# K's rows from split sums, the FFN gate's row inside the first block, and splits and copies at other places, in an adaLN, S4 and SwiGLU kernel

## The chip, the cores and the metric

The kernel runs on one core of one Trainium2 chip. The core has five engines with a queue of instructions each: TensorE (PE, matmuls; its weight loads are shown as PEld), VectorE (DVE), ScalarE (ACT), GpSimd (POOL) and SyncE (SP), which here only issues transfers. The metric is the device time of one execution in microseconds (us), the median of several runs. Matmuls write to PSUM, which is used here as eight banks of 128 x 512 fp32.

## The reference

One layer: an adaptive layer norm, a state space convolution (S4), a second adaptive layer norm and a SwiGLU FFN, with two residual sums. L = 2048 tokens, D = 448 channels, N = 256 states, F = 1792 hidden channels, all in fp32.

```python
mod = (_silu(c) @ w_mod).reshape(c.shape[0], 6, 1, -1)
sa, ca, ga, sb, cb, gb = (mod[:, 0], mod[:, 1], mod[:, 2], mod[:, 3], mod[:, 4], mod[:, 5])
h = _layernorm(x, axis=-1) * (1 + ca) + sa
x = x + ga * _A_ref(h, ...)      # y = conv(h, K) + h * Dskip, K[d, l] = Re sum_n C exp(dt A l) dt B
h = _layernorm(x, axis=-1) * (1 + cb) + sb
x = x + gb * ((_silu(h @ w_gate) * (h @ w_up)) @ w_down)
```

## The kernel before

**Method.** Where the exponents `dt A l` are small enough, K[d, l] is taken as a straight line in l: a value `m0` and a slope `m1` for each channel, both multiplied by the gate `ga`. The convolution is then two running sums over the tokens, made by matmuls with triangular matrices, and a sum carried from tile to tile in `run`. A flag computed from the states picks this path; otherwise a general path runs, which these inputs do not take.

**Precision.** A fp32 matmul runs as two records in the trace. Where that is too dear, an operand is split into a high part rounded to fp32r and a low part (the rest, also in fp32r), and the product is three fp32r matmuls of one record each: high x high, high x low, low x high. ACT makes the high part (a cast), DVE the low one (a subtraction).

**Stages.** The tokens are 16 tiles of 128, in blocks of 2, 2, 3, 3, 3, 3 tiles (`BLOCKS`). An opening stage prepares everything and makes the first two tiles ready; then for each block `ffn` runs over 14 slices f of the hidden channels. A step f is `gate_up(f)`, 22 matmuls (L724), and then `down(f - 1)`, 6 or 9 matmuls (L768). Its other work: `p`, the silu on ACT (L739); the product of gate and up on DVE (L752); its high part `phi` on ACT (L755) and its low part `plo` on DVE (L756). In the first block (`fresh`) the weights of the slices are split while it runs: `split_d(f)` (L112; ACT L115, DVE L117) and, with `nw`, `split_w(f + 2)` in three pieces (L119; ACT L123, DVE L125 and L127), mixed with the rest of the step.

**Order.** Each engine runs its instructions strictly in the order in which the program issues them. In the opening this order is written out by hand: `PLAN` is a list of short names, each standing for a function in `todo`, and `ORDER` is the order of the transfers that SP issues (s: states, m: columns of `w_mod`, x: tiles of tokens, w and d: weights of FFN slices). The names of `PLAN` that matter here:

- `pa`, `ps`: rows of the modulation as matmuls with c spread over 128 rows (`mod_part`). `gp`, `cp`, `sp`, `gq`: the same in four groups of 32 columns (`mod_quads`). `gt`, `gac`: the gate `ga` turned into columns.
- `S1`, `S20`, `S21`, `S3` (ACT), `a2`, `a3` (DVE): sums over the states. `t1` to `t5`, `wr`, `wi`: the products they need. `m0`, `dg`, `gdm` (POOL), `m1`: combining and gating them.
- `k0`, `k1`, `gdr`: the columns `m0`, `m1` and the skip `gdm` spread into rows by `row_of` (L348), matmuls against the unit matrix; `gd` copies the last.
- `h..`, `v0.`, `v1.`, `hd.`: the first norm of tiles 0 and 1 and its products with the rows; `o..`: the matmuls that sum them (`o00` to `o02` tile 0, `o10` to `o14` tile 1; `far` and `ramp` are constant matrices); `xh1`, `x1`: tile 1's residual.
- `st`, `r`, `n1.`, `xn`: the second norm of the two tiles (statistics on DVE, root on POOL L167 and L168, scaling on DVE and ACT). `tr`: its transposes, `hi` and `lo`: its split (ACT L428, DVE L433). `sbt`, `sbc`: the shift `sb` as columns, needed by `hi`.
- `l1`, `lr0`, `lr1`: the sum left over for the next tile; `lr1` ends with a transfer that ACT issues (L410, L411). `x0`: a copy of tile 0's residual.
- `gq`, `gqc`, `gbk`, `gb`: the gate row of the FFN: four groups, copied, summed and spread over 128 rows by one matmul with `pick` (`spread_row`, L381), copied to `gb`.
- `w0..`, `w1..`, `w2..`, `d0.`, `d1.`: splits of the first weights.

**In the blocks.** `TIMES` says at which half step (2f before `down`, 2f + 1 after it) the pieces of the next block's tiles are issued: for blocks 0 and 1 the last two entries are the root of the second norm and, per tile, `make_xn` (L189: DVE L193, ACT L194 and L195). At the end of a block the transposes of the next tiles (L206) follow the matmuls of f = 13 on PE.

Of the kernel before, what the change touches and what calls it, by code (L numbers as in the profile page):

```python
# [51 lines left out]
def f32(ap):  # L52
    return ap.bitcast(F32)
# [3 lines left out]
def tile_kernel(ctx, tc, x, a_re, a_im, b_re, b_im, c_re, c_im, log_dt,  # L57
# [13 lines left out]
    def bank():  # L71
        t = psg.tile([128, 512], F32, name="bank")
        return t
# [160 lines left out]
    def mod_part(ps, w, ks):  # L234

        for k in ks:
            if k < 3:
                pe.matmul(ps[:, 0:D], cs[:, k:k + 1].to_broadcast([128, 128]), w[:, k * D:(k + 1) * D],  # L238
                          start=k == 0, stop=False)
            else:  # L240
                for z in range(2):
                    pe.matmul(ps[:, z * D // 2:(z + 1) * D // 2], cs[:, 3 + z:4 + z].to_broadcast([128, 128]),
                              w[:, 3 * D:NM], start=False, stop=z == 1)

    def mod_quads(ps, w):

        for k in range(3):
            pe.matmul(ps[32 * k:32 * k + 32, 0:D], cs[:, k:k + 1].to_broadcast([128, 32]), w[:, k * D:(k + 1) * D],
                      start=True, stop=True)
        for z in range(2):  # L250
            pe.matmul(ps[96:128, z * D // 2:(z + 1) * D // 2], cs[:, 3 + z:4 + z].to_broadcast([128, 32]), w[:, 3 * D:NM],
                      start=z == 0, stop=z == 1)

    def to_dram(row, col):
# [12 lines left out]
    with tc.tile_pool(name="pre", bufs=1) as pre:  # L267
# [3 lines left out]
        wms, S = {5: m5.rearrange("p a b -> p (a b)")}, {}  # L271
# [32 lines left out]
        ident2 = pre.tile([128, 64], F32)  # L304
# [31 lines left out]
        qt = {n: pre.tile([128, D], F32, name="qt" + n) for n in "gcsb"}  # L336
        gdm = pre.tile([128, 4], F32, name="gdm")
        t_, WV = f32(tri), ve
# [8 lines left out]

        def row_of(m, ps, last=ident2):  # L348

            for k in range(4):  # L350
                n = 128 if k < 3 else 64
                pe.matmul(ps[:, k * 128:k * 128 + n], m[:, k:k + 1].to_broadcast([128, 128]), ident if k < 3 else last,
                          start=True, stop=True)
            return ps[:, 0:D]
# [3 lines left out]
        def row(g, z):  # L358

            if z == 0:  # L360
                psm[g] = bank()
            mod_part(psm[g], wms[g], (0, 1) if z == 0 else (2, 3))
# [21 lines left out]
        def gd_row():  # L384
            psm["d"] = bank()
            row_of(gdm, psm["d"], ident[:, 0:64])

        def scaled(o, a, b):
            po.tensor_tensor(o, a, b, op=OP.add)
            po.tensor_tensor(o, o, gac, op=OP.mult)  # L390

        def gated_dt():
            po.tensor_tensor(dt2, dt2, gac, op=OP.mult)
            po.tensor_tensor(ndt2[:, 2:4], ndt2[:, 2:4], gac[:, 2:4], op=OP.mult)
            po.tensor_tensor(a2[:, 0:2], a2[:, 0:2], gac[:, 0:2], op=OP.mult)
# [29 lines left out]
        def high(q):  # L425
            for k in range(4):
                c_ = slice(q * 128, (q + 1) * 128)
                sc.activation(hhi[:, k, c_], pk[q][:, k * 128:(k + 1) * 128], AF.Identity, bias=sbc[:, k:k + 1])  # L428
# [16 lines left out]
        def flag_of():  # L445
# [18 lines left out]
            "m0": do(scaled, m0, m0, m0_), "m1": add(m1, a1, a2), "dg": gated_dt, "k0": do(row_of, m0, CV), "k1": do(row_of, m1, DN[2]),  # L464
            "gdm": mul(gdm, vec[:, 8:12], gac, po), "gdr": gd_row, "gd": copy(gd, lambda: psm["d"][:, 0:D]),

            **{f"{n}{z}": do(row, g, z) for n, g in (("pa", 1), ("ps", 0)) for z in range(2)},
            **{n: do(quads, n[0] if n[1] == "p" else "b", g) for n, g in (("gp", 2), ("cp", 4), ("sp", 3), ("gq", 5))},
            **{n + "c": (lambda c, b: lambda: sc.copy(qt[c], psm[c][:, 0:D]))(c, b) for n, c, b in
               (("gp", "g", 0), ("cp", "c", 0), ("sp", "s", 0), ("gq", "b", 0))},  # L470
# [5 lines left out]
            "gbk": do(spread_row, "b"), "gb": copy(gb, lambda: psm["b"][:, 0:D]),  # L476
# [4 lines left out]
            **{f"hd{q}": mul(hd[q], h01[q], gd, po) for q in range(2)},  # L481
# [9 lines left out]
            **{f"tr{q}": do(to_channels, q) for q in range(2)}, **{f"hi{q}": do(high, q) for q in range(2)},  # L491
# [5 lines left out]
            "w2": do(split_w, 2, 0), "w21": do(split_w, 2, 1), "w22": do(split_w, 2, 2),  # L497
            **{f"d{j}{z}": do(split_d, j, z) for j in range(2) for z in range(2)},
# [201 lines left out]
    def run_blocks(pools, stages, first=None):  # L700
        work, hid = pools.work, pools.hid
        def ffn(ts, fresh, last, todo):
# [4 lines left out]
            def gate_up(f, nw):  # L707
                head = fresh and f == 0
                if fresh and f > 1:
                    split_d(f)  # L710
# [4 lines left out]
                ps = [DN[2] if head else bank(), bank()]  # L715
# [95 lines left out]
            for f in range(NF):  # L811
                gate_up(f, f + 2 if fresh and f and f + 2 < NF else None)
                if fresh:
                    pools.load(f + 2 + NS if f else NF, f + NS)
                if last and f in (2, 4):
                    gated(NF - 2 + (f == 4))
                for g, a in todo.get((f, 0), []):
                    g(*a)
                if f and not (last and f == NF - 1):
                    down(f - 1, qz)  # L820
                if last and f == NF - 2:
                    last_sums()
                for g, a in todo.get((f, 1), []):
                    g(*a)
# [8 lines left out]
        for j in range(NP0, NP0 + NS):  # L833
            pools.load(j)
# [10 lines left out]
        for b, ts in enumerate(TILES):  # L845
            todo = {}
            if b + 1 < len(TILES):
# [152 lines left out]
    with cond.Else():  # L1000
        y = general_conv()
        with ExitStack() as es:
            pools = Pools(es)
            run_blocks(pools, *general_path(pools, y))
# [60 lines left out]
```

## Time and profile before

| | |
|---|---|
| median of 3 runs | 488.02 us (487.7 to 488.93) |
| the profiled execution's own time | 489.08 us |
| its span, from the first instruction to the last | 487.3 us |
| PE busy | 474.4 us (97%) in 2743 matmul records |
| DVE busy | 284.7 us (58%) |
| ACT busy | 155.9 us (32%) |
| POOL busy | 60.8 us (12%) |
| clock granted to TensorE, mean | 0.996 |

A row of the timeline has the start and the length in us, the engine, the line of the kernel, the operation, the tile written and the tiles read, the shape, and how many like it were merged; in brackets the idle time of the engine before it and what ended it. A row of the chain of waits has start, length, engine, tile and line. An `x2` behind fp32 matmuls is one product in two records. The ends of matmuls are modelled, so the start-to-start distance of records tells their price better than their length.

### The profile page before, as it was taken

The numbers are of one execution on the slowest core, as the hardware profiler recorded it, in microseconds if no ns is written. First come the engines' busy times: TensorE is split into PE (matmuls) and PEld (weight loads), VectorE is DVE, ScalarE is ACT, GpSimd is POOL, SyncE is SP. The second block draws the span as 40 slices with busy tenths as digits, with TensorE's granted clock in tenths as the row PEclk, the third lists the DMA queues.
The fourth block names the chain that finished last, engine by engine and source line by source line (L and its number), as shares of the span: only waits on it lengthen the run. The fifth ranks groups of instructions, "written<-read, shape, count | busy, mean of one in ns | idle before, by whom it ended". The sixth has DMA issues, their size and how long they took to land.

```text
span 487.3 us, 7022 instructions
## 1 busy us (share of the span) xinstructions
PE 474.4 (97%) x2743; PEld 447.1 (92%) x2743; DVE 284.7 (58%) x549; ACT 155.9 (32%) x336; POOL 60.8 (12%) x83
## 2 busy tenths in 40 slices
PE   6998999999999999999999999999999999999996
PEld 4667988999998999999999999999999999999995
DVE  4978999577886446565654656264476635222225
ACT  4875555432225212232212133231222231211111
POOL 1231000000000040410004121002241000000000
PEclk9998999999999999999999999999999999999999
DMA  8953752030000200011120011130001112000001
GB/s 309 406 212 110 244 188 87 16 96 1 0 3 2 94 1 0 31 35 49 56 76 1 2 43 45 43 114 0 2 0 45 44 43 77 22 1 0 1 1 62
DMA packets 18778, 31.24 MB, mean 64 GB/s; under 512 B 2608, under 2 KB 13488, under 8 KB 18736
## 3 DMA queue, kind: packets, MB, share of 16 engines
q1 hardware_dynamic: 18000, 30.52, 18.4%
q8 instruction: 23, 0.38, 0.3%
q10 hardware_dynamic: 736, 0.19, 0.2%
q14 instruction: 19, 0.16, 0.1%
HBM read 24.61 MB, written 6.03 MB: 63 GB/s over the span
## 4 chain that ended last, share of the span: by engine, by line
PE 90%; DMA 3%; DVE 3%; ACT 2%; issue 1%; SPq 0%; ACTq 0%; DVEq 0%
PE bank L724 57%; PE dn L768 27%; DMA wm<-in_w_mod_groups_dram 2%; DMA x<-in_A_u_dram 1%; ACT raw L195 1%; PE dn L454 1%; PE bank L238 1%; PE bank L928 1%; PE cv L927 0%; DVE gu L125 0%; PE cv L929 0%; ACT gu L123 0%; DVE raw L193 0%; PE bank L206 0%; DVE hlo L433 0%
## 5 line engine op out<-in xcount | busy, mean ns | idle before, releaser
L724 PE MATMUL bank<-hhi,gu 128*128 128x384 f32 (+1 forms) x1169 | 212.4, 320 | 2.0 <-ACT gu L123 1.4
L724 PEld LDWEIGHTS bank<-hhi,gu 128*128 128x128 f32 x1169 | 192.0, 189 | 5.5 <-ACT gu L123 1.6
L724 PE MATMUL bank<-hlo,gu 128*128 128x384 f32 (+1 forms) x668 | 132.5, 320 | 0.0
L724 PEld LDWEIGHTS bank<-hlo,gu 128*128 128x128 f32 x668 | 110.7, 189 | 0.0
L752 DVE TENSOR_TENSOR bank<-raw,bank 128x384 f32<-128x384 f32 (+1 forms) x69 | 36.9, 534 | 125.0 <-PE bank L724 122.7
L755 ACT CAST phi<-bank 128x384 fp32r<-128x384 f32 (+1 forms) x83 | 36.9, 444 | 144.2 <-DVE bank L752 144.2
L739 ACT ACTIVATE raw<-bank 128x384 f32<-128x384 f32 (+1 forms) x70 | 32.9, 470 | 122.9 <-PE bank L724 114.8
L756 DVE TENSOR_TENSOR plo<-bank,phi 128x384 fp32r<-128x384 f32 (+1 forms) x83 | 42.5, 512 | 37.5 <-ACT phi L755 37.5
L768 PE MATMUL dn<-wdh,phi 128*128 128x448 f32 x218 | 58.3, 369 | 0.0
L768 PE MATMUL dn<-wdh,plo 128*128 128x448 f32 x218 | 57.7, 366 | 0.0
L768 PE MATMUL dn<-wdl,phi 128*128 128x448 f32 x218 | 57.6, 365 | 0.0
L768 PEld LDWEIGHTS dn<-wdl,phi 128*128 128x128 f32 x218 | 41.0, 188 | 3.5
L768 PEld LDWEIGHTS dn<-wdh,plo 128*128 128x128 f32 x218 | 40.9, 188 | 3.3
L768 PEld LDWEIGHTS dn<-wdh,phi 128*128 128x128 f32 x218 | 39.0, 189 | 2.1 <-ACT run L951 0.7
L167 POOL TENSOR_SCALAR rsb<-mvb 128x1 f32<-128x1 f32 (+2 forms) x13 | 4.6, 354 | 172.2 <-DVE mvb L151 170.5
L167 POOL TENSOR_SCALAR rsa<-mva 128x3 f32<-128x3 f32 (+1 forms) x6 | 1.4, 233 | 120.9 <-DVE mva L151 120.9
L123 ACT CAST gu<-raw 128x1024 fp32r<-128x1024 f32 x14 | 14.6, 1044 | 1.1 <-DVE run L410 1.1
L125 DVE TENSOR_TENSOR gu<-raw,gu 128x768 fp32r<-128x768 f32 x14 | 13.3, 953 | 1.8 <-ACT gu L123 1.8
L916 DVE TENSOR_TENSOR vl<-m,vh 128x448 fp32r<-128x448 f32 x12 | 9.1, 757 | 6.7 <-ACT vh L915 6.1
L902 POOL TENSOR_TENSOR m<-m,gm 128x448 f32<-128x448 f32 x9 | 10.4, 1153 | 21.0 <-DVE m L184 17.2
L117 DVE TENSOR_TENSOR wdl<-rawd,wdh 128x448 fp32r<-128x448 f32 x16 | 9.9, 621 | 3.4 <-ACT wdh L115 3.2
L194 ACT ACTIVATE raw<-raw,rsb 128x64 f32<-128x64 f32 x14 | 4.8, 346 | 21.0 <-DVE raw L193 11.9
(232 smaller groups left out, 416.0 us busy)
## 6 DMA issues: line engine op xcount, KB each, us to landing
raw<-in_B_w_gate_up_dram SPq DMA_DIRECT2D x14, 512.0 KB, 3.7
rawd<-in_B_w_down_dram SPq DMA_DIRECT2D x16, 224.0 KB, 3.8
x<-in_A_u_dram SPq DMA_DIRECT2D x12, 224.0 KB, 3.0
out_dram<-x SPq DMA_DIRECT2D x11, 224.0 KB, 2.0
xd<-raw SPq DMA_DIRECT2D x9, 256.0 KB, 2.0
raw<-xd SPq DMA_DIRECT2D x36, 64.0 KB, 2.0
wm<-in_w_mod_groups_dram SPq DMA_DIRECT2D x5, 448.0 KB, 8.2
wm<-in_w_mod_groups_dram SPq DMA_DIRECT2D x5, 336.0 KB, 8.2
```

The costliest lines, as they stand in the source:

```text
L117: ve.tensor_tensor(lo, wdn[j], f32(hi), op=OP.subtract)
L123: sc.copy(wgu[j][:, :, 0:4, :], w)
L125: en.tensor_tensor(lo, w[:, :, 0:3, :], f32(hi), op=OP.subtract)
L167: po.tensor_scalar(rs[:, 0:n], self.mv[:, 0:n, 1], EPS, None, op0=OP.add)
L724: pe.matmul(ps[s][:, 0:n], w[:, s, a], (hlo if lo else hhi)[:, k, 0:n], start=first and q == 0, stop=end and q == len(ka) - 1)
L739: sc.activation(p[:, 0:n], ps[0][:, 0:n], AF.Silu)
L752: ve.tensor_tensor(ps[1][:, 0:n], p[:, 0:n], ps[1][:, 0:n], op=OP.mult)
L755: sc.copy(hi[:, 0:n], ps[1][:, 0:n])
L756: ve.tensor_tensor(lo[:, 0:n], ps[1][:, 0:n], f32(hi[:, 0:n]), op=OP.subtract)
L768: pe.matmul(dn[q][:, 0:D], u[:, cs], v, start=f == 0 and z == 0, stop=f == (NF - 3 if last else NF - 1) and z == 2)
L902: (ve if on_v else po).tensor_tensor(v, h, g, op=OP.mult)
L916: ve.tensor_tensor(vl, v0, f32(vh), op=OP.subtract)
```

## The change

It has five parts.

1. **Rows as fp32r products.** `row_of` takes each sum as two halves (high in fp32r and rest) and adds two fp32r matmuls per group of 128 channels, against a unit matrix in fp32r, instead of one fp32 matmul. `parts_of` makes the halves: on POOL for `m0` and the skip, on DVE for `m1`.
2. **The gate row of the FFN** is no longer in `PLAN`. `end_gate(0)` (the four groups into the bank `CV`, a copy to `gb`) is issued at half step 2 of the first block and `end_gate(1)` (the spreading matmul, the copy) at half step 4.
3. **Splits of the next weights.** The split of w1 and d0 moves ahead of `lr0`, `x0` and `lr1`; the splits of w2 and d1 leave the opening and are made in steps f = 0 and f = 1 of the first block like the later ones; f = 1 uses the order of matmuls that only f = 0 had (high parts of the weights first). The transfers of w1 and d0 go ahead of the gate's columns.
4. **The order of the opening.** `gt` and `gac` earlier, `ps` in three pieces, `gdr` before `cp`, `o00`, `o10` and `o12` earlier, the gating of `a2` apart, `hi0` in two halves, `hd1` on DVE instead of POOL.
5. **Late copies.** `make_xn` at half steps 22 and 23 instead of 24 and 23 in block 0, and at 23, 24, 24 instead of 25, 25, 25 in block 1, whose root moves from 25 to 23.

```diff
-    ((1, 1), 5, ((5, 10, 15, 15, 15), (9, 9, 18, 19, 19)), 19, (24, 23)),
-    ((2, 3, 3), 3, ((5, 6, 8, 10, 10, 11, 13), (7, 8, 14, 15, 17, 17, 18), (13, 17, 17, 18, 20, 21, 21)), 25, (25, 25, 25)),
+    ((1, 1), 5, ((5, 10, 15, 15, 15), (9, 9, 18, 19, 19)), 19, (22, 23)),
+    ((2, 3, 3), 3, ((5, 6, 8, 10, 10, 11, 13), (7, 8, 14, 15, 17, 17, 18), (13, 17, 17, 18, 20, 21, 21)), 23, (23, 24, 24)),
...
-ORDER = """sf x0 x1 sc m10 se sd m11 m20 m21 m00 sb m01 sa m40 m41 m30 m31 w0 m50 m51 d0 w1 d1 x2 w2 x3 d2"""
-PLAN = """t4 pa0 t1 S1 t2 pa1 t3 wi ca gp S20 wr ps0 h00 gpc h01 S21 gt a2 gac sq1 ps1 m0 gdm dg t5 k0 S3 h10 cp v00 a3 gdr
-m1 k1 cpc gd h11 hd0 v01 ck sq0 v10 hd1 o00 cbw v11 o01 o02 xh1 gc0 sa st0 o10 o12 o13 o14 fs w0 r0 n10 sp xn0 x1 st1 gq r1 fl n11 gc1 spc
-tr0 gqc sbt xn1 sbc w01 l1 tr1 gbk hi0 w02 lo0 hi1 lo1 gb lr0 x0 lr1 w1 w11 w12 d00 d01 w2 w21 w22 d10 d11"""
+ORDER = """sf x0 x1 sc m10 se sd m11 m20 m21 m00 sb m01 sa m40 m41 m30 m31 w0 w1 d0 m50 m51 d1 x2 w2 x3 d2"""
+PLAN = """t4 pa0 t1 S1 t2 pa1 t3 wi ca gp S20 wr ps0 h00 gpc gt h01 S21 psx gac a2 sq1 ps1 m0 dg gdm t5 k0 gdr S3 h10 cp v00 dga a3 o00
+o10 m1 k1 cpc gd h11 hd0 v01 ck sq0 v10 cbw o12 v11 w0 o01 o02 hd1 o13 o14 xh1 gc0 sa st0 fs sp r0 n10 spc x1 xn0 gc1 st1 sbt tr0 sbc r1
+fl n11 l1 hi00 xn1 w01 tr1 hi01 w02 hi1 lo0 lo1 w1 w11 d00 w12 lr0 d01 x0 lr1"""
...
+    def end_gate(z):
+        if z:
+            pe.matmul(CV[:, 0:D], pick.to_broadcast([128, 128]), gb, start=True, stop=True)
+        else:
+            mod_quads(CV, gate_w)
+        sc.copy(gb, CV[:, 0:D])
...
+        def parts_of(o, m, en):
+            en.tensor_copy(o[:, 0], m)
+            en.tensor_tensor(o[:, 1], m, f32(o[:, 0]), op=OP.subtract)
...
-                pe.matmul(ps[:, k * 128:k * 128 + n], m[:, k:k + 1].to_broadcast([128, 128]), ident if k < 3 else last,
-                          start=True, stop=True)
+                for z in range(2):
+                    pe.matmul(ps[:, k * 128:k * 128 + n], m[:, z, k:k + 1].to_broadcast([128, 128]),
+                              identr if k < 3 else last, start=z == 0, stop=z == 1)
...
         def scaled(o, a, b):
             po.tensor_tensor(o, a, b, op=OP.add)
             po.tensor_tensor(o, o, gac, op=OP.mult)
+            parts_of(ms[0], o, po)
+
+        def slope_of():
+            ve.tensor_tensor(m1, a1, a2, op=OP.add)
+            parts_of(ms[1], m1, ve)
+
+        def gated_skip():
+            po.tensor_tensor(gdm, vec[:, 8:12], gac, op=OP.mult)
+            parts_of(gd2, gdm, po)
...
-            **{f"hd{q}": mul(hd[q], h01[q], gd, po) for q in range(2)},
+            **{f"hd{q}": mul(hd[q], h01[q], gd, (po, ve)[q]) for q in range(2)},
...
-                head = fresh and f == 0
-                if fresh and f > 1:
+                head = fresh and f < 2
+                if fresh and f:
                     split_d(f)
...
-                gate_up(f, f + 2 if fresh and f and f + 2 < NF else None)
+                gate_up(f, f + 2 if fresh and f + 2 < NF else None)
                 if fresh:
-                    pools.load(f + 2 + NS if f else NF, f + NS)
+                    pools.load(f + 2 + NS, f + NS)
...
-        for j in range(NP0, NP0 + NS):
+        for j in range(NP0, NP0 + NS - 1):
             pools.load(j)
...
                     go(EXTRA[0], gate_0)
+                    go(2, end_gate, 0)
+                    go(4, end_gate, 1)
```

More of the change, by code (lines that the diff above doesn't have):

```diff
@@ L302, in tile_kernel @@
         ve.tensor_copy(all1, ones.to_broadcast([128, 128]))
-        ident2 = pre.tile([128, 64], F32)
+        ident2 = pre.tile([128, 64], F32R)
+        identr = pre.tile([128, 128], F32R)
+        ve.tensor_copy(identr, ident)
         ve.tensor_tensor(ident2, ident[:, 0:64], ident[:, 64:128], op=OP.add)
@@ L423, in branch_1, with high @@
             ve.tensor_tensor(xs[1], os[1], hd[1], op=OP.add)
-        def high(q):
-            for k in range(4):
+        def high(q, ks=range(4)):
+            for k in ks:
                 c_ = slice(q * 128, (q + 1) * 128)
@@ L714, in gate_up @@
                 lo = hid.tile([128, MB * 128], F32R, name="plo")
-                ps = [DN[2] if head else bank(), bank()]
+                ps = [DN[2] if fresh and f == 0 else bank(), bank()]
                 top = [(k, a) for k, ws in enumerate(((0, 4), (1, 5), (2, 6), (3,))) for a in ws]
@@ L1000, in tile_kernel @@
     with cond.Else():
+        for z in range(2):
+            end_gate(z)
         y = general_conv()
```

35 lines of the change are left out of this document (19 added, 16 removed).

## The prediction, made before the changed kernel ran

> **What bounds the kernel now.** I read first the chain of work that ended last, from the page.
>
> ```profile
> span 487.3 us, 7022 instructions
> PE 90%; DMA 3%; DVE 3%; ACT 2%; issue 1%; SPq 0%; ACTq 0%; DVEq 0%
> ```
>
> TensorE is nearly the whole chain, so only what shortens PE's queue or removes one of its waits can be seen at the end. Next I read that chain in order of time. Here is the opening stage and the first steps of the first FFN block (start, length, what).
>
> ```profile
> 20.09 0.84 PE cv L352 x8
> ...
> 26.54 0.75 PE dn L484 x2
> ...
> 28.78 0.76 PE bank L248 x4
> ...
> 35.64 0.64 DVE run L410
> 36.30 0.61 ACTq L411
> 36.95 1.05 ACT gu L123
> 38.03 0.97 DVE gu L125
> 39.05 3.92 PE bank L724 x21
> 42.98 1.76 PE dn L768 x6
> 44.74 2.61 PE bank L724 x22
> ...
> 48.57 2.61 PE bank L724 x22
> ```
>
> Up to about 34 us PE works through the plan without a pause. Then the chain leaves it: a row of `run` on DVE (L410), the transfer that ACT issues for it (36.30), and only behind that ACT's cast of w1 (36.95) and DVE's low part of w1 (38.03). Step f=1 of the FFN begins at 39.05 and takes 3.92, where f=2 takes 2.61; down(0) behind it takes 1.76, where a full step of 3.83 (44.74 to 48.57) leaves 1.22. From f=3, at 48.57, PE alone carries the chain. That is the mark against which I measure the start.
>
> The windows say why f=1 is slow (window, length, then busy time of PE, PEld, DVE, ACT, POOL; then the clock granted).
>
> ```profile
> 36.60:39.00 2.40, 0.45 (x2) 0.19 (x1) 0.96 (x1) 2.05 (x3) 0.00 (x0) 1.00 0.01 2
> 40.20:41.80 1.60, 1.60 (x10) 1.60 (x9) 1.55 (x3) 0.00 (x0) 0.00 (x0) 0.50 0.70 154
> ```
>
> After 2.4 us nearly without matmuls the clock is 0.50. So w1's lateness costs 2 us of idleness (2.40 - 0.45) and 1.85 of slow matmuls (3.92 - 2.61 + 1.76 - 1.22). With neither, f=2 would begin nearly 4 us before 44.74.
>
> **The rows as fp32r products.** K's row (`k0`), the slope's (`k1`) and the skip row (`gdr`) were 8 matmul records each (four fp32 products, two records apiece), 0.84 us for the first. They become eight fp32r products, again 8 records. A record of 128 columns in fp32r is not in the trace; the nearest are the last ones of 192 columns.
>
> ```profile
> 481.71 0.25 PE L796 MATMUL dn<-wdh,phi 128*128 128x192 f32 x1
> ...
> 482.25 0.28 PE L796 MATMUL dn<-wdh,plo 128*128 128x192 f32 x1
> ```
>
> Six start within 0.54, one each 0.11. I take 0.11, since 192 columns are hardly cheaper than that and the weights have 128 columns in both: 0.88 a row, which is no gain to speak of. Bounds: if the step shrinks with the columns, 0.11 x 128/192 = 0.07, a row takes 0.58 and the three gain 0.8 to 1.1; if a split product costs a whole fp32 one (two records of 0.12), a row takes 1.9 and the three lose 3.0.
>
> The halves are made by two more small operations for each sum: on POOL for `k0` and `gdr`, on DVE for `k1`. POOL's have a price that shows here.
>
> ```profile
> 19.01 1.10 DVE L452 TENSOR_TENSOR t<-sa,t 128x896 f32<-128x896 f32 x1 [0.34 <-DMA sa<-in_A_states_dram]
> 19.13 1.05 POOL L393 TENSOR_TENSOR dt<-dt,gac 128x4 f32<-128x4 f32 x1
> ```
>
> A POOL operation on four columns takes 1.05: it ends when a DVE operation with two SBUF operands ends. In the new plan `gac` is out 0.7 earlier (the turn `gt` goes ahead of the second product of `ps`), but a2, which reads SBUF twice, now runs behind it beside POOL. The second half for `k0` may stick behind `t5` until 20.2. I charge 0.15.
>
> **The opening's new order.** PE: `gdr` before `cp`, then o00 and o10 before `k1`, o12 before o01 and o02; the gate's quads (0.76) and its spreading product (0.75, like `ck`) leave. Added up from 20.25: k0 0.88, gdr 0.88, cp 0.85 (quads, and their first load), k1 0.88, o00, o10, ck, o12 and o01 0.75 each like the two fp32 records of L484, o02 0.2 as one fp32r record gives 27.7 for the end of tile 0's sum, which was 26.54. Tile 1's ends at 28.1, 0.4 behind it (far and ramp), instead of 28.45. So what lengthens is the way from the first sum: DVE has `hd1` now (it was POOL's) and runs through both tiles without a pause.
>
> ```profile
> 27.53 0.69 DVE L437 SCALAR_TENSOR_TENSOR h<-dn,mvb,cbw 128x448 f32<-128x448 f32 x1
> 28.56 0.62 DVE L423 TENSOR_TENSOR x<-dn,hd 128x448 f32<-128x448 f32 x1 [0.34 <-PE dn L454]
> ...
> 30.20 0.66 DVE L437 SCALAR_TENSOR_TENSOR h<-x,mvb,cbw 128x448 f32<-128x448 f32 x1
> 31.32 0.67 ACT L490 ACTIVATE h<-h,rsb 128x448 f32<-128x448 f32 x1 [0.59 <-POOL rsb L168]
> 32.13 2.18 ACT L428 ACTIVATE hhi<-bank,sbc 128x128 fp32r<-128x128 f32 x8
> 33.45 2.16 DVE L433 SCALAR_TENSOR_TENSOR hlo<-bank,sbc,hhi 128x128 fp32r<-128x128 f32 x8
> 34.17 0.57 ACT L455 COPY gb<-bank 128x448 f32<-128x448 f32 x1
> ```
>
> Tile 0's statistics and n10 took 1.68 from its sum on (26.54 to 28.22), and from x1's start to n11's it was 1.64. From 27.7 that makes x1 at 29.4 and n11, with `sbc` now ahead of it, at 31.15, 0.95 later than 30.20. ACT's second xn, 1.12 behind n11, moves from 31.32 to 32.25. From its end to the last `hi` it was 2.3 with part of tile 0's `hi` in it; I take 1.85: 34.75 (was 34.31). On DVE w01 and w02 (1.42) follow n11 (0.66) at once, where they waited for `sbc`, and `lo` (2.16) ends at 35.4 (was 35.61). FFN's f=0 ends about where it did, 36.7: its last eight matmuls wait for `hlo`. The two gate products leave PE here without a gain, because PE waits for tile 1 instead.
>
> **The first steps of the FFN.** DVE's queue there, before:
>
> ```profile
> 40.02 0.95 DVE L125 TENSOR_TENSOR gu<-raw,gu 128x768 fp32r<-128x768 f32 x1
> ...
> 41.44 0.63 DVE L117 TENSOR_TENSOR wdl<-rawd,wdh 128x448 fp32r<-128x448 f32 x1
> 42.09 0.43 DVE L752 TENSOR_TENSOR bank<-p,bank 128x256 f32<-128x256 f32 x1
> 42.96 0.42 DVE L756 TENSOR_TENSOR plo<-bank,phi 128x256 fp32r<-128x256 f32 x1 [0.44 <-ACT phi L755]
> 43.30 0.68 DVE L698 SCALAR_TENSOR_TENSOR gm<-g,ntok,gm 128x448 f32<-128x448 f32 x1
> ...
> 45.38 0.41 DVE L752 TENSOR_TENSOR bank<-p,bank 128x256 f32<-128x256 f32 x1
> ```
>
> The cast of w1 now precedes lr0, x0 and the transfer: 34.7 to 35.75 on ACT; its low parts on DVE at 35.8 to 37.2 (1.42, from 40.02 to 41.44 above). PE needs them behind six high products of f=1, so f=1 runs 36.7 to 39.3 at full clock. That removes the stall. What is late next: DVE does d01 (0.6) and lr1 (0.6) until 38.35; ACT stands at lr1's transfer until then, and behind it in ACT's queue are p of f=0 (at 39.0: the transfer's issue took 0.65, from 36.30 to 36.95; PE has been done since 36.7), the cast of w2 (39.3 to 40.3) and phi. On DVE: f=0's product at 39.4, w2's low part at 40.35 (it waits for the cast), plo, the rest of w2: 42.15. Then `gate_0` and two statistics, 43.30 to 45.38 before, 2.08; d1, which left the opening, 0.55; f=1's product at 44.8. It stood at 45.38: DVE, which has the same work to do and idles 1.7 in both, is only 0.6 ahead.
>
> PE: quads of the gate 39.3 to 40.05, down(0) from phi at 40.65 to 42.1, f=2 to 44.7. Now the added wait: the spreading product reads `gb`, and ACT copies `gb` only behind phi of f=1, which waits for the product at 44.8: phi to 45.65 (plo followed the product by 0.87, 42.09 to 42.96), the copy, up to 0.57, to 46.1. PE stands 1.4 us with down(1) and f=3 queued behind. Spreading 0.75 and a load of 0.2: 47.05; down(1) 1.22: f=3 begins at 48.3 instead of 48.57. **First term: -0.25.** Afterwards PE's step of 3.83 is longer than DVE's, so the lead stays. Without the hold PE would be at f=3 by 46.7, a gain of 1.9; if DVE's lead falls away too, the term is +0.3. The transfers of w1 and d0 go before m5 on SP's queue; each has over 8 us until it is read, so this costs nothing, and no wait on that queue is lengthened.
>
> **The late copies.** At the seams of blocks 0/1 and 1/2 PE's transposes wait for the normalised tiles (the bracket is PE's idle time and what ended it).
>
> ```profile
> 95.61 0.66 PE L206 MATMUL bank<-ident,raw 128*128 128x128 f32 x4 [0.42 <-ACT raw L195]
> ...
> 151.91 0.67 ACT L195 ACTIVATE raw<-raw,rsb 128x448 f32<-128x448 f32 x1
> ...
> 152.63 0.33 PE L206 MATMUL bank<-ident,raw 128*128 128x128 f32 x1 [0.19 <-ACT raw L195]
> ...
> 152.85 0.67 ACT L195 ACTIVATE raw<-raw,rsb 128x448 f32<-128x448 f32 x1
> ...
> 153.57 0.66 PE L206 MATMUL bank<-ident,raw 128*128 128x128 f32 x4 [0.61 <-ACT raw L195]
> ```
>
> In block 0 both copies now sit at f=11 (half steps 22 and 23; one was at 24), nearly a step sooner: the whole 0.42 goes. In block 1 they sit at 23, 24, 24 (all were at 25). One copy then passes ACT during f=11, but pushes p of f=12 back by about half of its 0.94, and two copies remain behind f=12's low part, 0.94 each (151.91 to 152.85). The last is ready 0.45 sooner, out of the 0.8 that PE waits. **Second and third term: -0.42 and -0.45**; if p's delay eats them, the sum loses 0.5.
>
> **Sum:** -0.25 - 0.42 - 0.45 = -1.1. The profiled execution took 489.08 with a span of 487.3; its own time would become 488.0. The median of the runs is 488.02, so 486.9 there.
>
> **Rivals.**
> 1. *The rows are cheap* (0.07 a record, or DVE otherwise a microsecond earlier). Everything behind tile 0's sum moves 1.1 ahead, `gb` with it: f=3 at 47.2, in all -2.2: 485.8. For it: fewer columns in the stream. Against: 0.11 at 192.
> 2. *A split product costs a whole fp32 one*: slower. Place: k0, gdr, k1, all before tile 0's sum. Price 3.0 on a chain that DVE carries to f=3; less the three terms of 1.1: +1.9, 489.9. It turns slower once a row takes over 1.25. Against it: the 192-column rows.
> 3. *POOL is starved.* The second root on POOL (r1) meets n11, w01, w02, three DVE operations with two SBUF operands, with nothing between. If it gets in only after w02, the xn of tile 1 slips 1.4 (w01 and w02), and the rest of the start with it: 488.3. Against it, from block 2:
>
> ```profile
> 196.70 0.69 DVE L193 SCALAR_TENSOR_TENSOR raw<-x,mvb,cbw 128x448 f32<-128x448 f32 x1
> 196.75 0.72 POOL L167 TENSOR_SCALAR rsb<-mvb 128x1 f32<-128x1 f32 x1 [13.70 <-DVE mvb L151]
> 197.30 0.60 DVE L907 TENSOR_TENSOR m<-m,run 1x448 f32<-1x448 f32 x1
> ```
>
> POOL ended at 197.47 though the next DVE operation followed at once: it waits for one operation, not for a row of them. The Trainium skill (SBUF — State Buffer, "Who interferes with whom") says that whichever operation issues first holds the shared pair for its whole length and the other blocks fully; the trace agrees with the blocking, and by that rule alone r1 could be passed again and again, as in this rival.
>
> 4. *The clock falls again.* PE stands 0.6, 0.2 and 1.4 between 40 and 46. If that makes slow matmuls as it did before, 1.85 is lost: 488.75. For it: the drop came after a stretch that was not free of matmuls (0.45 of 2.40, then f=1's first ones). The Trainium skill (TensorE: Matmul & The Clock Gate, "The HAM clock gate") asks for an idle window of about 3.4 us; here the clock fell after less, so the rule is milder than the row; by it alone this rival has no chance.
>
> **How the numbers follow.** Forecast 0.48, rival 1 0.27, rival 2 0.09, rival 3 0.08, rival 4 0.08. A measurement here tells a change from none at about 0.3%, 1.46 us: below 486.56 is faster, above 489.48 slower. The forecast's own range, 486.0 to 487.8 (late copies lost, or half the hold gone), has a fifth of its weight below 486.56. Faster: 0.27 + 0.10 = 0.37. Slower: rival 2 and a quarter of 3 and 4, 0.13. The same: 0.50. Range 484.9 to 489.8: rival 1 with 0.9 of its own spread, to just below rival 2.
>
> **What would show it.** k0, gdr and k1 of 8 records at 0.11; f=1 at 2.6 with the clock at 1.00; ACT's p of f=0 directly behind lr1's transfer; PE idle about 1.4 before the product that reads `gb`; f=3 near 48.3; no wait at the first seam and some 0.5 less at the second. It is wrong if the rows' records lie at 0.07 or 0.24, if p of f=0 comes before 38.5 or after 40, or if the gate's copy isn't what PE waits for.

## The result, and the profile after

| | before | after |
|---|---|---|
| median of 9 runs each, same chip | 487.97 us (487.54 to 488.93) | 489.63 us (489.26 to 490.08) |
| ratio after / before | | 1.0031, 95% interval 1.0021 to 1.0042 |
| profiled execution: time, span | 489.08, 487.3 us | 490.08, 488.1 us |

The changed kernel is slower by 1.5 us (1.0 to 2.0), where 1.1 us less had been forecast.

Two executions cannot be laid over each other from their first instruction. The transfer `m00`, which the first product of `ps` waits for, lands more than a microsecond earlier or later from one execution to the next (that product began between 14.34 and 16.16 us in the thirteen profiled executions of this study), and everything behind it moves along. This is that product in the timeline of the kernel before:

```profile
15.91 1.77 PE L238 MATMUL bank<-wm,cs 128*128 128x448 f32 x4
```

and in the timeline of the changed one:

```profile
14.80 1.02 PE L238 MATMUL bank<-wm,cs 128*128 128x448 f32 x2 [0.18 <-DMA wm<-in_w_mod_groups_dram]
```

So all marks below count from the start of this product, "after m00". The chain of waits of the changed kernel (start, length, what) has the rest:

```profile
PE 93%; DMA 2%; ACT 1%; DVE 1%; POOL 1%; issue 1%; DVEq 0%; POOLq 0%
...
30.45 1.86 POOL rsb L168
...
47.63 0.55 ACT gb L262
48.23 1.02 PE cv L259 x2
...
50.45 2.61 PE bank L753 x22
...
100.38 5.28 PE bank L753 x44
...
158.26 7.74 PE bank L753 x44
```

PE has 93% of the chain where it had 90%: it is busier on the chain, and later. f = 3 begins at 50.45, 35.65 after m00; before it was 48.57, 32.66 after m00. **The start lost 3.0 us.** From f = 3 to block 1 the changed kernel takes 49.93, and from there to block 2 57.88; the chain of the kernel before has for the same two:

```profile
48.57 2.61 PE bank L724 x22
...
99.25 5.23 PE bank L724 x44
...
157.32 7.72 PE bank L724 x44
```

50.68 and 58.07. **The late copies gained 0.75 and 0.19.** 3.0 less 0.94 is 2.05, at the upper end of what the runs' times say (1.0 to 2.0).

The loss lies between the statistics of tile 1 and the first `p` of the FFN. The changed kernel's timeline there, engines mixed (in brackets the idle time before a row and what ended it):

```profile
30.34 0.66 DVE L466 SCALAR_TENSOR_TENSOR h<-x,mvb,cbw 128x448 f32<-128x448 f32 x1
30.45 1.85 POOL L168 TENSOR_TENSOR rsb<-rsb,mhalf 128x1 f32<-128x1 f32 x1
30.93 0.94 DVE L125 TENSOR_TENSOR gu<-raw,gu 128x768 fp32r<-128x768 f32 x1
31.91 0.42 DVE L127 TENSOR_TENSOR gu<-raw,gu 64x256 fp32r<-64x256 f32 x1
...
32.33 0.67 ACT L519 ACTIVATE h<-h,rsb 128x448 f32<-128x448 f32 x1 [0.92 <-POOL rsb L168]
...
33.05 0.90 PE L391 MATMUL bank<-ident,h 128*128 128x128 f32 x3 [1.71 <-ACT h L519]
...
34.63 1.14 ACT L457 ACTIVATE hhi<-bank,sbc 128x128 fp32r<-128x128 f32 x4 [1.12 <-PE bank L394]
...
35.80 1.13 DVE L462 SCALAR_TENSOR_TENSOR hlo<-bank,sbc,hhi 128x128 fp32r<-128x128 f32 x4 [1.13 <-ACT hhi L457]
...
38.93 0.63 DVE L439 TENSOR_TENSOR run<-run,dn 32x448 f32<-32x448 f32 x1
39.59 0.61 ACTq L440 DMA_DIRECT2D run<-run  x1
...
41.18 0.39 ACT L768 ACTIVATE p<-dn 128x256 f32<-128x256 f32 x1 [2.91 <-PE bank L753]
41.65 0.43 DVE L781 TENSOR_TENSOR bank<-p,bank 128x256 f32<-128x256 f32 x1 [2.09 <-ACT p L768]
```

Three things are to be seen. POOL's second operation of tile 1's root (one column) takes 1.85 and ends at 32.30. In the kernel before it took 0.84 and ended 0.43 behind n11 (31.29 and 30.86); here it ends not 0.43 behind n11 (31.00) but 0.43 behind w01 (31.87), the longer DVE operation that follows n11 at once. w02 (31.91) no longer holds it. PE then stands 1.71. And between the transfer of `lr1` (issued by 40.20) and `p` there is a microsecond in which ACT runs nothing. What is in it shows a view of one line, the one that loads the flag by which the program branches into the blocks; each engine loads it for itself; this is ACT's row (engine, operation, duration in ns, start in us):

```profile
L535 ACTq TENSOR_LOAD <-flag x1: 703/703/703, 40.2 to 40.2; - x1
```

The same line of the kernel before:

```profile
L506 ACTq TENSOR_LOAD <-flag x1: 609/609/609, 37.0 to 37.0; - x1
```

There it lay under the cast of w1 (36.95 to 38.0) and cost nothing. In the changed kernel the casts of w1 and d0 come before the transfer and those of w2 and d1 behind the branch, so nothing covers the 0.70.

Last, the windows (window, length, busy time of PE, PEld, DVE, ACT, POOL, then the clock granted):

```profile
31.40:35.10 3.70, 1.53 (x7) 0.80 (x7) 2.02 (x6) 1.66 (x6) 0.90 (x1) 0.69 0.46 116
35.10:39.80 4.70, 4.66 (x22) 4.69 (x23) 3.67 (x8) 3.12 (x7) 0.00 (x0) 0.52 0.21 42
39.80:42.40 2.60, 2.60 (x24) 2.58 (x22) 0.43 (x1) 1.22 (x3) 0.00 (x0) 1.00 0.44 167
```

PE's pause before tile 1 is followed by a stretch at half clock in which f = 0 runs. What that costs in the whole time is not shown: of the nine executions of the changed kernel two had a mean clock of 0.999 and took 489.70 and 489.97, the other seven had 0.992 to 0.995 and took 489.26 to 490.08.

### The profile page after: what moved, and what is told of

Same layout as the page of the kernel before. It is cut to its first block, busy times and chain, and to the rows that moved or that the text cites. A ratio compares the mean times of both kernels' runs of the same rounds, so it can differ in the third digit from the quotient of the medians.

```text
span 488.1 us, 7029 instructions
## 1 busy us (share of the span) xinstructions
PE 475.0 (97%) x2743; PEld 447.4 (92%) x2743; DVE 285.3 (58%) x553; ACT 155.5 (32%) x336; POOL 61.5 (13%) x86
## 4 chain that ended last, share of the span: by engine, by line
PE 93%; DMA 2%; ACT 1%; DVE 1%; POOL 1%; issue 1%; DVEq 0%; POOLq 0%
PE bank L753 59%; PE dn L797 27%; DMA wm<-in_w_mod_groups_dram 2%; DMA vec<-in_c_log_dt_dram 1%; PE dn L753 1%; PE dn L483 1%; PE bank L959 1%; PE cv L958 0%; PE cv L960 0%; ACT sca L360 0%; PE bank L972 0%; POOL rsb L168 0%; DVE x L836 0%; PE bank L206 0%; PE cv L971 0%
## 5 line engine op out<-in xcount | busy, mean ns | idle before, releaser
L167 POOL TENSOR_SCALAR rsa<-mva 128x3 f32<-128x3 f32 (+1 forms) x6 | 2.4, 396 | 119.2 <-DVE mva L151 119.2
L933 POOL TENSOR_TENSOR m<-m,gm 128x448 f32<-128x448 f32 x9 | 10.4, 1155 | 21.4 <-DVE m L184 17.5
L952 POOL TENSOR_TENSOR m<-m,gd 128x448 f32<-128x448 f32 x9 | 11.5, 1282 | 0.0
```

The source lines that it names most:

```text
L167: po.tensor_scalar(rs[:, 0:n], self.mv[:, 0:n, 1], EPS, None, op0=OP.add)
L933: (ve if on_v else po).tensor_tensor(v, h, g, op=OP.mult)
L952: (ve if on_v else po).tensor_tensor(h, h, gd, op=OP.mult)
```

## The experiments

The ratios are to runs of the kernel before on the same chip (three chips; its medians there were 487.97 to 488.04). The mark f = 3 is read in the chain of one profiled execution of each kernel, so a gain in the mark is a gain of the typical run only where the ratio shows it too. How far marks scatter shows one pair: the kernel before and d1_copies have the same opening, and their marks differ by 0.27. The parts by themselves come first, then cures of the changed kernel, then versions meant to beat both.

| run | f=3 after m00 | median | ratio to before, 95% interval |
|---|---|---|---|
| before | 32.66 | 487.97 | |
| after | 35.65 | 489.63 | 1.0031, 1.0021 to 1.0042 |
| d1_copies | 32.39 | 486.91 | 0.9976, 0.9967 to 0.9985 |
| d1_rows | 33.94 | 489.60 | 1.0033, 1.0021 to 1.0044 |
| d2_rows | 33.05 | 488.55 | 1.0011, 0.9998 to 1.0024 |
| d1_splits | 35.26 | 489.77 | 1.0035, 1.0021 to 1.0049 |
| u1_root | 34.57 | 489.38 | 1.0026, 1.0017 to 1.0036 |
| u2_gate | 34.37 | 488.86 | 1.0025, 1.0014 to 1.0036 |
| u3_sp | 34.82 | 488.23 | 1.0001, 0.9987 to 1.0016 |
| u5_all | 30.81 | 485.90 | 0.9954, 0.9937 to 0.9971 |
| v1_copies_sp | 31.17 | 486.28 | 0.9970, 0.9955 to 0.9984 |
| v2_late_splits | 30.09 | 485.20 | 0.9941, 0.9923 to 0.9959 |
| v3_first_cast | 28.58 | 483.82 | 0.9914, 0.9896 to 0.9933 |

### The late copies alone (d1_copies)

The kernel before with the two lines of `TIMES` from the change and nothing else.

> The kernel before with the late copies alone (make_xn at half steps 22 and 23 in block 0; 23, 24, 24 and the root at 23 in block 1). Between the first block's f=3 and the third block the changed kernel lost 0.9 to 1.0 us less than the kernel before, so both theories expect about -0.9: 487.0 to 487.3, with no wait of PE at the first seam (0.42 before) and about 0.6 left at the second (0.8 before). If the gain belongs to something else, the time is that of before.

The median falls by 1.1, a little more than expected. f = 3 to block 1 takes 49.93 and block 1 to block 2 57.85, the lengths of the changed kernel. So the copies did all that they could in the change too, and the loss is in the other parts. This run also shows something of the start that it shares with the kernel before. Its first steps of the FFN (timeline, PE alone):

```profile
38.29 0.39 PE L724 MATMUL bank<-hhi,gu 128*128 128x256 f32 x1 [1.38 <-ACT gu L123]
39.28 0.98 PE L724 MATMUL bank<-hhi,gu 128*128 128x256 f32 x6 [0.61 <-DVE gu L125]
...
43.22 0.67 PE L768 MATMUL dn<-wdh,phi 128*128 128x448 f32 x2 [1.18 <-ACT phi L755]
```

and its windows:

```profile
36.80:39.20 2.40, 0.49 (x2) 0.19 (x1) 0.93 (x1) 2.01 (x3) 0.00 (x0) 1.00 0.03 10
39.20:42.00 2.80, 2.72 (x21) 2.56 (x21) 2.69 (x6) 1.20 (x3) 0.00 (x0) 1.00 0.41 92
```

PE stands as long before f = 1 as in the kernel before, but here the clock stays at 1.00 behind it. f = 1 is done sooner, and PE waits 1.18 for phi instead: f = 3 gains 0.27 of the 1.85 that the slow matmuls seemed to cost. What sets f = 3 is phi of f = 0, that is DVE's product for f = 0, and not PE's stall.

### The rows alone, in two orders (d1_rows, d2_rows)

The kernel before with `parts_of`, the fp32r unit matrices and the new `row_of`; the second run changes POOL's order as well, as the change does:

```diff
-... ps1 m0 gdm dg t5 k0 S3 ...
+... ps1 m0 dg gdm t5 k0 S3 ...
```

> The kernel before with the rows as fp32r products of split sums alone, in the old order of the opening. Prediction's step: eight records of 0.11, the time of before within 0.3 us (487.7 to 488.3). If the rows or their halves on POOL carry the loss, 489 or more, and the rows' records lie at 0.13 or more or start late.

> The kernel of before with the rows as fp32r products alone, with dt's gating ahead of the skip row's sum on POOL (in the first run of the rows it stood behind it). Theory (the rows' records cost what the fp32 ones did; the first run's loss was POOL's order): S3 begins 4.4 us after m00's landing (5.36 in the first run, 4.30 before), f=3 at 33.0 (33.94; 32.66 before); median 488.2. Rival (the halves or the split products themselves cost it): f=3 at 33.8 or later, median 489.5.

POOL's timeline in the first run:

```profile
18.18 1.04 POOL L353 CAST ms<-m 128x4 fp32r<-128x4 f32 x1
19.30 0.20 POOL L354 TENSOR_TENSOR ms<-m,ms 128x4 fp32r<-128x4 f32 x1
19.45 0.20 POOL L406 TENSOR_TENSOR gdm<-vec,gac 128x4 f32<-128x4 f32 x1
...
20.14 0.20 POOL L410 TENSOR_TENSOR dt<-dt,gac 128x4 f32<-128x4 f32 x1
```

The first half sticks behind DVE's `t5` (1.04 for four columns), and the four small operations behind it come ahead of `dt`, for which ACT's sums S3 wait: these begin 5.36 after m00 (20.37), where the kernel before had them 4.30 after m00 (20.21). With `dg` first, f = 3 comes at 33.05 instead of 33.94. So 0.9 of the 1.3 lost was POOL's order, which the change avoids. The first run took 489.60, where the prediction's step had meant at most 488.3; the second came near what was expected of it (33.0). The records are no cheaper and hardly dearer than forecast; here is `gdr` in the second run:

```profile
20.95 1.08 PE L361 MATMUL bank<-identr,gd 128*128 128x128 f32 x8
```

Eight records within about a microsecond, as the fp32 ones. What is left, 0.4 in the mark and 0.6 in the median, has an interval that just includes no change; this part gains nothing and may cost about 0.4.

### The earlier splits alone (d1_splits)

```diff
-... hi1 lo1 gb lr0 x0 lr1 w1 w11 w12 d00 d01 w2 w21 w22 d10 d11
+... hi1 lo1 gb w1 w11 d00 w12 lr0 d01 x0 lr1 w2 w21 w22 d10 d11
```

The splits of w2 and d1 stay in the opening, so this is half of the change's third part.

> The kernel before with the splits of w1 and d0 ahead of lr0, x0 and lr1, and the splits of w2 and d1 left in the opening behind lr1. Cover theory (the casts behind lr1's transfer hide the load of the flag that ACT does at the branch between the opening and the FFN; the change took them away): the stall before f=1 goes and nothing takes its place, f=3 begins 1 to 2 us sooner, 486.0 to 487.0. Rival (DVE's total work sets f=3 in any order): less than 0.4 sooner, 487.6 to 488.1.

The chain of waits:

```profile
36.94 0.64 DVE run L410
37.60 0.61 ACTq L411
38.25 1.05 ACT gu L123
...
42.29 2.61 PE dn L768 x6
44.90 4.19 PE bank L724 x22
...
50.31 2.61 PE bank L724 x22
```

and its windows behind f = 1:

```profile
39.60:42.30 2.70, 0.01 (x1) 0.01 (x1) 2.19 (x5) 0.88 (x4) 0.00 (x0) 0.86 0.27 39
42.30:45.00 2.70, 2.70 (x8) 2.44 (x9) 2.63 (x7) 1.16 (x2) 0.07 (x1) 0.50 0.65 247
```

The stall before f = 1 is gone, as the prediction had it, and neither theory's time came: f = 3 is 2.6 later and the median 1.7 slower. ACT still stands at `lr1`'s transfer, the next cast (38.25) stands behind it, and f = 0's product comes 26.4 after m00, where it was 26.2 (42.09). PE's wait only moved behind f = 1 and became one piece (3.68); the half clock now falls on down(0), 2.61 for 1.76, and on f = 2, 4.19 for 2.61, with no wait left to hide it. These two make 2.4 of the 2.6. The other executions agree: the three with a mean clock of 0.992 took 490.21 to 491.24, the five with 0.994 or 0.995 489.02 to 489.83. A wait removed on PE is worth nothing while ACT's and DVE's queue sets the next step.

### The root passed on POOL (u1_root)

The changed kernel with w01 and w02 behind tile 0's low parts, so that POOL's root has only n11 beside it:

```diff
-fl n11 l1 hi00 xn1 w01 tr1 hi01 w02 hi1 lo0 lo1 w1 ...
+fl n11 l1 hi00 hi01 lo0 xn1 tr1 w01 w02 hi1 lo1 w1 ...
```

> The changed kernel with w01 and w02 moved behind lo0 and xn1, so that POOL's second root meets only one DVE operation with two SBUF operands (n11) instead of n11 and w01 back to back. Starved-root theory: the root takes 0.85 instead of 1.85, xn of tile 1 comes 1 us sooner, PE idles less before tr1 and keeps its clock, lo ends 1.5 to 2 us sooner, f=3 1.2 to 1.9 sooner: 487.9 to 488.5. Rival (the load of the flag behind lr1's transfer and DVE's queue set p of f=0 and f=1's product): under 0.5 us, 489.2 to 489.6.

POOL's timeline:

```profile
30.68 0.97 POOL L168 TENSOR_TENSOR rsb<-rsb,mhalf 128x1 f32<-128x1 f32 x1
```

0.97 for 1.85, and f = 3 comes 1.08 sooner. So the root was held by two DVE operations in a row. All thirteen profiled executions agree: in the three where w01 follows n11 at once the operation takes 1.84 or 1.85, in the other ten 0.83 to 0.97, and in each it ends 0.4 behind the operation that held it. The time does not confirm the gain: the median, 489.38, is the rival's and not the theory's, and the interval overlaps that of the changed kernel. In the profiled execution, the slowest of its nine (490.71), the gain is lost again at the end: from the last sum (483.05) to the end of the span (488.7) it takes 5.65, where the changed kernel has 4.2. That is one execution; why the median did not follow the mark stays open. In this run's chain the flag load stands openly:

```profile
38.69 0.61 ACTq L440
39.35 0.71 ACTq L535
```

### The gate's row back in the opening (u2_gate)

```diff
-fl n11 l1 hi00 xn1 w01 tr1 hi01 w02 hi1 lo0 ...
+fl n11 gq l1 hi00 gqc xn1 gbk w01 tr1 hi01 gb w02 hi1 lo0 ...
...
-                    go(2, end_gate, 0)
-                    go(4, end_gate, 1)
```

> The changed kernel with the gate's row made in the opening again: its quads behind n11's transposes of tile 0, the spreading product in the pause of PE before tile 1 is turned, the copy gb in ACT's pause before tile 1's hi; nothing of it is left in the first block. Theory (the copy behind phi of f=1 holds PE): no wait for gb and no quads in the block, so down(1) follows phi of f=1 at once and f=3 begins 1.4 us sooner, 34.2 us after m00's landing (35.65 in the changed kernel); median 488.2. Rival (ACT and DVE set f=1's product and PE would stand for phi anyway, or the opening pays for the two products): f=3 at 35.3 or later, median 489.5.

f = 3 comes at 34.37, 1.28 sooner, near what the theory had. But not all of it is the hold by `gb`. PE's and ACT's timelines:

```profile
33.01 0.49 PE L391 MATMUL bank<-ident,h 128*128 128x128 f32 x3
33.43 0.44 PE L394 MATMUL bank<-ident,h 128*64 128x128 f32 x4
...
40.48 0.38 ACT L769 ACTIVATE p<-dn 128x256 f32<-128x256 f32 x1 [2.90 <-PE bank L754]
```

The root on POOL is passed here too (1.84), yet PE does not stand before tile 1: the gate's two products fill the pause, and the transposes and f = 0 run at full clock. So p of f = 0 begins 25.82 after m00, 0.56 sooner than in the changed kernel; only the other 0.72 can be the hold in the block, which the changed kernel's trace has as 0.73. The time shows less: the median is 0.8 below that of the changed kernel, but the ratios to the kernel before, 1.0025 and 1.0031, have intervals that overlap.

### lr1's transfer on another queue (u3_sp)

```diff
                 ve.tensor_tensor(run0[e], run1[e], os[1][e], op=OP.add)
-                sc.dma_start(run[0:1], run[127:128])
...
         for j in range(NP0, NP0 + NS - 1):
             pools.load(j)
+        if first is None:
+            sy.dma_start(run[0:1], run[127:128])
```

> The changed kernel with the transfer of lr1's row issued by SP at the start of the first block, behind its first weight loads, and not by ACT. Theory (ACT stands for lr1, then issues, and only then loads the flag, all in front of p of f=0): the flag is loaded at 23.5 us after m00's landing (25.44 in the changed kernel), p of f=0 begins at 25.2 as soon as PE has f=0 (26.38), f=0's product at 25.6 (26.85) and f=3 1.2 us sooner, 34.4; median 488.4. Rival (the half-clocked f=0 and DVE's queue set it, the copy gb holds PE at the same place): p moves less than 0.3 or f=3 stays within 0.3 of 35.65; median 489.6.

The flag load of ACT and, in ACT's timeline, p of f = 0:

```profile
L534 ACTq TENSOR_LOAD <-flag x1: 467/467/467, 34.3 to 34.3; - x1
```

```profile
39.06 0.38 ACT L767 ACTIVATE p<-dn 128x256 f32<-128x256 f32 x1 [1.14 <-PE dn L752]
```

With no transfer in front of it the load is made at 34.3, while ACT still has tile 1's `hi`, two casts and two copies to do: earlier than expected, and free. p begins 24.2 after m00 instead of 26.4 and now waits for PE alone, whose f = 0 runs at half clock. f = 3 gains 0.83 rather than 1.2: DVE has f = 1's product 2.2 sooner (29.95 for 32.11 after m00), but PE is then at the limit of its own queue and no longer stands for `gb`. So the transfer, with the load behind it, cost the changed kernel 0.8 by the mark and 1.4 in the median. This is the one single cure whose ratio lies clear of the changed kernel's: the time is that of the kernel before.

### All three cures (u5_all)

The edits of u2_gate and u3_sp, with this end of `PLAN`:

```diff
-fl n11 l1 hi00 xn1 w01 tr1 hi01 w02 hi1 lo0 lo1 w1 w11 d00 w12 ...
+fl n11 gq l1 hi00 hi01 lo0 xn1 gqc tr1 gbk w01 w02 hi1 lo1 w1 gb w11 d00 w12 ...
```

> The changed kernel with the three single cures at once: w01 and w02 behind tile 0's lo, so that the root of tile 1 isn't passed; the gate's row in the opening; the transfer of lr1's row on SP. Theory (three separate losses): the gains seen singly add up, 1.08 + 1.28 + 0.83, so f=3 begins 32.5 us after m00's landing (35.65 in the changed kernel, 32.66 before); with the late copies' gain of about 1.0 the median is 486.7. Rival (they hide the same loss, each removes what the next one would have shown): f=3 at 33.8 or later, median 488 or more.

f = 3 at 30.81: 4.84 sooner than in the changed kernel, where the three single gains add up to 3.19. So the cures do not hide one another; together they give more than the sum. The 1.65 beyond it goes along with the clock: this run's mean is 0.999, and f = 0 runs at full speed, since PE's pause before tile 1 is now 0.30; p of f = 0 begins 22.60 after m00, 1.61 sooner than in u3_sp, where it stood 1.14 for PE at half clock. No run here takes that apart further, and the new order of the opening was not run without the other parts. 485.90 is clearly below the changed kernel and below the kernel before; but the second part of the change is undone in it.

### Versions from the kernel before (v1_copies_sp, v2_late_splits, v3_first_cast)

The first has the late copies and SP's transfer. The second makes the splits of w2 and d1 in the block too, as the change does. The third also puts w1's cast ahead of the copies and of `lr1`, and `gate_0` and two statistics one half step later:

```diff
-    ((1, 1), 5, ...
+    ((2, 2), 5, ...
-EXTRA = (1,)
+EXTRA = (2,)
-... hi1 lo1 gb lr0 x0 lr1 w1 w11 w12 d00 d01
+... hi1 lo1 w1 gb w11 w12 lr0 d00 x0 lr1 d01
```

> The kernel of before with the late copies of the change and with the transfer of lr1's row issued by SP in the first block. Theory (that transfer on ACT's queue is what made w1's cast late): w1 is cast right behind x0, f=1 begins 21.4 us after m00's landing (23.14 before), no or one window of half clock, f=0's product at 24.4 (26.18), f=3 at 30.4 (32.66); median 484.6, below both kernels. Rival (the wait only moves behind f=1, as with the splits ahead of lr1): f=1 early, but PE stands over 2 us before down(0), f=3 at 32.2 or later; median 486.5.

> The kernel of before with the late copies, with the transfer of lr1's row on SP, and with the splits of w2 and d1 in the first block behind f=0's product, as the change has them. Theory (f=0's product stands behind w2's and d1's low parts on DVE, 2.0 us): f=0's product at 23.0 us after m00's landing (24.95 without the last part), no wait of PE before down(0), f=3 at 29.9 (31.17); median 485.1. Rival (w2's splits behind the product only make f=2 late, as DVE has the same work to do): f=3 at 30.9 or later, median 486.2.

> As the run before it (copies, SP's transfer, splits of w2 and d1 in the block), and with w1's cast and low parts ahead of the copies gb, lr0, x0 and of lr1, and with gate_0 and the two statistics one step later. Theory (ACT's and DVE's order alone set the first steps): no wait of PE before f=1 nor before down(0) nor down(1), f=0's product at 22.4 after m00's landing and f=3 at 28.7; median 483.9. Rival (DVE's work up to f=3 is the bound, whatever its order): f=3 at 29.8 or later, as in the run before it; median 485.

The first gained 1.2 on the copies alone in the mark and 0.6 in the median, a difference that lies within the two intervals; expected had been 2.0 in the mark and 484.6. DVE's timeline has the reason:

```profile
37.70 0.95 DVE L125 TENSOR_TENSOR gu<-raw,gu 128x768 fp32r<-128x768 f32 x1
...
39.12 0.63 DVE L117 TENSOR_TENSOR wdl<-rawd,wdh 128x448 fp32r<-128x448 f32 x1
39.77 0.43 DVE L751 TENSOR_TENSOR bank<-p,bank 128x256 f32<-128x256 f32 x1
```

The product of f = 0 stands behind the low parts of w2 and d1, 2.0 us (37.70 to 39.77) that nobody needs yet. With these in the block the product comes 23.0 after m00 (24.95 in the first) and f = 3 moves to 30.09, near the 29.9 expected. In the third f = 3 is at 28.58 (28.7 expected), and from 29 us on the steps of its chain up to f = 5 are PE's alone. 483.82 us, ratio 0.9914 (0.9896 to 0.9933), is the fastest kernel of this study.

## Why the prediction was wrong, point by point

The steps of the prediction and what the trace has, both counted from m00 (the predicted ones less 15.91, the measured less 14.80):

| step | predicted | measured | late by |
|---|---|---|---|
| end of tile 0's sum | 11.8 | 12.2 | 0.4 |
| n11 begins | 15.2 | 15.5 | 0.3 |
| second xn begins | 16.3 | 17.5 | 1.2 |
| last `hi` ends | 18.8 | 21.0 | 2.1 |
| `lo` ends | 19.5 | 22.1 | 2.6 |
| p of f = 0 | 23.1 | 26.4 | 3.3 |
| f = 0's product | 23.5 | 26.9 | 3.4 |
| f = 1's product | 28.9 | 32.1 | 3.2 |
| f = 3 | 32.4 | 35.65 | 3.3 |

- **The step that failed is "the opening's new order", and with it the first term, -0.25, which measured +3.0: the prediction let POOL's root in behind n11 and put p of f = 0 directly behind `lr1`'s transfer.** Up to n11 it holds within 0.4. Then come 0.9 at the root, 0.9 from xn to `hi`, 0.5 from `hi` to `lo` and 0.7 from `lo` to p. From p of f = 0 on every step is right again within 0.2, only 3.3 late. This division is that of one execution. In the times of many runs only the transfer together with the load behind it is confirmed by a cure of its own (u3_sp), the load not apart from it; the rest is confirmed only in the sum (u5_all).
- *The root (0.9).* This was rival 3, at 0.08, with the mechanism as written, but not to its end: the root was passed by w01 and not by w02. The evidence against it, one place in block 2 where POOL came in behind a single operation, was no rule; the operation that followed there works on a single partition (1x448). The Trainium skill (SBUF — State Buffer, "Who interferes with whom") says that the order of issue decides who blocks; the 1.85 beside 0.97 with w01 moved away agrees with being passed, and the 0.72 of the prediction shows that it need not happen.
- *From xn to `hi` (0.9).* The half clock, rival 4, came at a place the prediction did not look at: behind PE's pause of 1.71. Tile 1's transposes took 0.90 and 0.70 where the same two take 0.49 and 0.44 in u2_gate at full clock, some 0.6. The pause comes from the late root, but also from a sentence of the prediction: that the gate's two products leave PE "without a gain". They had been filling that pause; u2_gate, with them back, has the late root and no half clock. The other 0.3 was the estimate of 1.85, too short.
- *From `hi` to `lo` (0.5).* The prediction let `lo` overlap with `hi` as before. In the new plan tile 1's `lo` begins when the last `hi` ends and then takes 1.13.
- *From `lo` to p (0.7).* "ACT's p directly behind lr1's transfer" left out the flag load and branch that lie there. Moving the casts away from behind the transfer took their cover. The prediction asked what hides each edit, but not what the moved casts had been hiding.
- *The rows.* Right: records of 0.10 to 0.13, no gain. The price of POOL's halves was right in kind (1.15 for one of them behind `t5`), and the first run of the rows shows what the order there is worth, 0.9.
- *The start of the FFN.* f = 1 without a stall, DVE's five microseconds from product to product and the hold by `gb` came out as worked out: 5.26 for 5.4 between the products, and from the product of f = 1 to f = 3 3.54 for 3.5. The hold appears in the trace as 0.73 before the product that reads `gb`, not 1.4, since f = 2 ended later.
- *What the stall was worth.* The opening remark that without the stall and the slow matmuls f = 2 would begin nearly 4 us earlier was wrong: d1_copies has no slow matmuls and gains 0.27, d1_splits has no stall and loses 2.6. In both PE then waits for phi of f = 0. The sum did not use this figure, since it went by DVE.
- *The late copies.* -0.87 forecast, -0.94 measured, but otherwise divided: 0.75 and 0.19 for 0.42 and 0.45. At the second seam PE still waits, in the changed kernel's timeline:

```profile
154.47 0.66 PE L206 MATMUL bank<-ident,raw 128*128 128x128 f32 x4 [0.61 <-ACT raw L195]
```

The last copy is ready no sooner against PE than before. The first seam gave more than its wait of 0.42 because the eight transposes behind the wait also took longer in the chain: 1.17 before (95.61 to 96.78), 0.87 without the wait (97.07 to 97.94).

That the time lay within the range was luck: its upper end came from rival 2, another mechanism. The chance of slower, 0.13, was too small. Three rivals that each shift the same chain were priced as if only one could come, and two of them came together in the profiled execution, the second partly caused by the first.

## What to carry to other kernels

When a piece of work is moved off a queue, ask what it was covering there: a flag load, a branch or a transfer's issue becomes visible when the casts beside it leave. A wait of the busiest engine is worth only the distance to the next wait behind it, so follow the side engines' queue to the first product before pricing a stall; here taking one transfer off ACT's queue and two splits off DVE's, in front of that product, brought f = 3 forward by 2.3 (d1_copies to v2_late_splits), where the whole change put it back by 3.0. Weigh a mark of one profiled execution against the times of many runs before calling it a gain. And lay two profiled executions over each other at a common event, not at their first instruction.

## What the runs showed of the hardware that was not expected

- The same stall of PE (0.45 and 0.49 us of matmuls within 2.40) was followed by half clock in the kernel before and by full clock in d1_copies. The Trainium skill (TensorE: Matmul & The Clock Gate, "The HAM clock gate") describes the activity windows as free-running, about 3.4 us long, so that the outcome depends on where in a window the work falls; these two runs of the same opening agree with that, though no run here shows the window itself. The prediction had read the drop of one execution as a fixed cost.
- An engine's load of the branch flag took 0.46 to 0.71 us. Behind compute operations ACT makes it ahead of time, at 34.3 in u3_sp with 3.6 us of its work still to come; behind a transfer that waits, at 40.2, only once that has been issued. The Trainium skill (Perfetto Trace Analysis, "Sequencer Loop") says that the sequencer pushes engine instructions into a queue and carries out control instructions itself, which fits both rows.
- The second operation of the root on POOL, on one column, took 0.57 us for tile 0 beside n10, which reads a sum from PSUM; for tile 1 it took 0.83 to 0.97 beside one DVE operation with two SBUF operands, and 1.84 or 1.85 beside two in a row. In all thirteen profiled executions tile 1's ended 0.4 behind the last of those that held it.
